# An attention-and-MLP kernel on one core: a diagonal's matmuls as a step of their own, one broadcast by a casting transfer, and a reordered opening list

## The chip, the core and the metric

The kernel runs on one core of one Trainium2 chip. The core has engines that each work through an instruction queue of their own, in order, and wait for one another by semaphores: PE (TensorE, matmuls), DVE (VectorE), ACT (ScalarE), POOL (GpSimd) and SP (SyncE, which here only issues transfers). DMA engines move data between memory and the core. The metric is device time in microseconds (us), from the start to the end of one execution; lower is better.

## What is computed

The reference has two parts. The first is a linear attention with a decay `w` for each head and channel and a bonus `u` for the current token, over 4 sequences of 768 tokens, 8 heads of 48 channels:

```python
for t in range(S):
    cur = einsum('bhd,bhe->bhde', u[None] * k[t], v[t])
    y[t] = einsum('bhd,bhde->bhe', r[t], state + cur)
    state = w[None, :, :, None] * state + einsum('bhd,bhe->bhde', k[t], v[t])
```

The second takes y, with the heads side by side, as x of 3072 tokens by 384 columns: `h = x @ w_in` (384 by 2048), `g = maximum(0.01 * h, h)`, `out = g @ w_out` (2048 by 384).

## The kernel before

**Stages.** The tokens are cut into 24 stages of 128 tokens (n = 0 to 23); four consecutive stages are the same chunk of the four sequences. Inside a chunk the recurrence becomes matrix products: scaled copies of r and k are turned (channels onto partitions), a 128 by 128 score matrix is made for each head and masked, and y is the scores times v, plus r times the state carried from the chunk before, plus a diagonal term, in which each token's v is multiplied by the sum of r, k and u over the channels. Two stages make a pair m, whose 256 tokens go through the MLP together. From m = 3 on (stages 6 and later in the MLP, 10 and later in the attention) a loop emits the work; everything before is emitted in the order of a hand-written list, the string ORDER.

**The list.** Each word in ORDER emits one step, with the number of its stage:

- `k`, `r`, `v`: load of one 128 by 384 piece, from fp32 in memory to bf16 on the chip, issued by POOL (line 223); `wi`, `wo`: load of a quarter of w_in or w_out, also by POOL (lines 233 and 237). k0 and r0 alone go by ACT and SP.
- `P`: DVE multiplies r (`q`) or k (`k`) by its decay table into qk (line 353). `T`: PE turns one half of qk with four matmuls (line 407). `t`: the copy of it from PSUM to tp, by ACT (line 421), or by DVE where `@` stands behind (line 419). `X8T` to `X11T`: for these stages a DMA transpose issued by SP takes the place of T and t (line 358).
- `A`: the scores, 8 matmuls into two PSUM banks (line 432). `M`: the mask, by DVE, one bank at a time (line 441; line 445 from stage 8 on).
- `X` with a number alone: DVE's product of the two halves of tp (line 368); `D`: its sums over channels, four small matmuls (line 460), into spare columns of the PSUM bank that y will use; `Q`: for stages 0 to 7 DVE multiplies v by these sums into vs (line 375). From stage 8 on `q` is DVE's three operations on r, k and the table u_tab (lines 382, 384, 386), and `Q` is two multiplications of the identity by POOL (line 393), which put the sums on the diagonal of the score tile before the mask is applied.
- `Y`: the sum of y in PSUM (line 566); for stages 0 to 7 it begins with three matmuls of vs with the identity (line 559). `y`: ACT's copy of it to xT (line 580).
- `K`: k times v (line 473); `S`: DVE's new state from it (lines 531, 534, 536).
- `G n.g` and `g`: a quarter of the first MLP product for one stage, 12 matmuls (line 605), and ACT's leaky ReLU of it (line 615). `J m.j` and `j`: an eighth of it for a pair of stages, 6 matmuls of 256 columns (line 628), and its ReLU (line 638). `H`: the second product for one stage, 16 matmuls of 384 columns (line 652); `h`: ACT's copy (line 664) and the store, issued by SP (line 666).
- `F`: fills, matmuls of ones whose result nobody reads (line 261), as many as the number says.
- The rest makes the tables: `w`, `w8`, `u8`, `u` are small loads by SP; `bc`, `lnw`, `qtab`, `ktab` the decay tables; `id8`, `wu8`, `Cm`, `Wl`, `C`, `W` the columns of w and of w times u; `u16`, `U`, `utab` a cast of the row u by ACT (line 326), a matmul that spreads it over the partitions (line 330), and a copy to u_tab by ACT (line 335).

**What sets the order.** A step's place in ORDER is its place in its engine's queue, and nothing moves it later. The class Sched notes for each step which buffers it reads and writes, and makes it wait for the steps before that wrote or read them. PSUM has eight banks; a step that needs one takes the one that has been free longest, so it also waits for the copy that freed it. There are no priorities: a step that waits holds everything behind it on its engine. The loads that are needed first in the loop, those of stages 12 and 13, stand at the end of the list; the loop's own loads are held back to a step of the MLP, those of the list are not.

After the list PE's first step is J3.0, the first eighth of the MLP for stages 6 and 7.

Of the kernel before, what the change touches and what calls it, by code (L numbers as in the profile page):

```python
# [17 lines left out]
HD = H * D  # L18
# [109 lines left out]
def bass_rwkv5_eagle__then__act_leaky_relu_kernel(  # L128
# [13 lines left out]
    def SB(name, shape, dt=BF16):  # L142
        return ctx.enter_context(nc.sbuf_tensor(name, shape, dt))
# [180 lines left out]

    def u_cast():
        add("act", lambda: A.activation(u_row16[:, :], u_row[:, :], AF.Copy), R=["u_row"], W=["u_row16"])

    def u_spread():
        ps_u, key = u_bank["u"] = take()
        add("pe", lambda: PE.matmul(ps_u[:, 0:HD], ones[0:1, 0:128], u_row16[:, :], start=True, stop=True),  # L330
            R=["ones", "u_row16"], W=[key])

    def u_table():
        ps_u, key = u_bank["u"]
        add("act", lambda: A.activation(u_tab[:, :], ps_u[:, 0:HD], AF.Copy), R=[key], W=["u_tab"])
        give(key)

    u_bank, c_bank = {}, {}
    at_bank, kv_bank, y_bank = {}, {}, {}
# [199 lines left out]
    def y_mm(n, ps_y, key):  # L539
        it, ia, iv, is_ = n % NTP, n % NAT, n % NVS, n % NT  # L540

# [13 lines left out]
        def emit():  # L555
            whole = n < DIAG
            if whole:
                for s in range(NSL):
                    PE.matmul(ps_y[:, 128 * s:128 * s + 128], vs[iv][:, 128 * s:128 * s + 128], ident[:, :],  # L559
                              start=s == 0, stop=False)  # L560
            columns = [sum((strip(s, q) for s in range(NSL)), []) for q in range(4)]
            for step in range(max(len(x) for x in columns)):
                for q in range(4):
                    if step < len(columns[q]):
                        s, a, m = columns[q][step]
                        last = PE.matmul(ps_y[32 * q:32 * q + 32, 128 * s:128 * s + 128], a, m,  # L566
                                         start=not whole and step == 0, stop=step == len(columns[q]) - 1)
# [90 lines left out]
    def g2_out(n, c0=0, c1=HD):  # L658
# [135 lines left out]
```

## Time and profile before

| | us |
|---|---|
| runs (3): median, lowest, highest | 171.94, 170.69, 172.17 |
| span of the profiled execution, first to last instruction | 168.6 |
| PE busy in it | 163.7 |
| DVE busy | 106.9 |
| POOL busy | 103.6 |
| ACT busy | 90.8 |
| PE's first matmul of J3.0, that is, the end of the list | 53.36 |

The span is the profiled execution's own time as the profile shows it; the page gives no device time beside it. The median of the runs is 3.3 us longer than the span; what lies around the first and the last instruction is not in the trace. Times in the trace are counted from the first instruction. A matmul's row is longer than its share of PE, because matmuls overlap: the distance from one group's start to the next is what a group costs. Durations in the chain of waits are such distances already.

### The profile page before, as it was taken

The page shows a single profiled execution, that of the slowest core. Times are in us where ns is not written, and L with a number is a line of the kernel's source. Part 1 is how long each engine was busy: PE and PEld are TensorE (multiplying, and loading weights), DVE is VectorE, ACT ScalarE, POOL GpSimd, SP SyncE. Part 2 cuts the span into 40 slices and gives each one's busy share as a digit, 9 for nine tenths or more (in the row PEclk, how much of TensorE's full clock was granted, in tenths as well). Part 3 has the DMA queues.
Part 4 walks back from the last instruction along what each step waited for, and adds up shares of the span by engine and source line. Part 5 has one row for each costly group of instructions (what it writes and reads, how often), then busy time and mean ns, then how long its engine had stood idle before and what let it go on. Part 6 is the DMA issues. An engine that isn't in the chain of part 4 may idle for free.

```text
span 168.6 us, 5011 instructions
## 1 busy us (share of the span) xinstructions
PE 163.7 (97%) x2170; PEld 126.1 (75%) x2170; DVE 106.9 (63%) x217; ACT 90.8 (54%) x167; POOL 103.6 (61%) x117
## 2 busy tenths in 40 slices
PE   6899999999999999999999999999999999999994
PEld 4787898988667867867867867768768668668663
DVE  6599799874583999869959959969876050000000
ACT  3837866886123933933834735735637538449221
POOL 7999999990249998994993993993708100000000
PEclk9999999999999999999999999999999999999999
DMA  6999999999999959999599399299241011011012
GB/s 99 142 151 165 170 167 173 182 184 148 130 167 187 163 75 144 155 118 173 71 140 167 64 141 177 71 132 193 59 121 47 0 51 47 0 51 47 29 68 95
DMA packets 99148, 19.67 MB, mean 117 GB/s; under 512 B 92339, under 2 KB 99126, under 8 KB 99126
## 3 DMA queue, kind: packets, MB, share of 16 engines
q0 software_dynamic: 76512, 10.03, 92.1%
q1 hardware_dynamic: 21574, 9.12, 23.2%
q8 instruction: 17, 0.28, 0.7%
q10 hardware_dynamic: 1040, 0.20, 0.6%
q14 instruction: 5, 0.04, 0.1%
HBM read 20.45 MB, written 4.72 MB: 149 GB/s over the span
## 4 chain that ended last, share of the span: by engine, by line
PE 89%; POOL 5%; DMA 4%; issue 0%; ACT 0%; POOLq 0%
PE ps L652 37%; PE ps L628 31%; PE ps L605 6%; PE ps L566 6%; DMA w_in_sb<-in_moe_w_in_dram 4%; PE ps L432 4%; PE ps L473 2%; POOL k_sb L223 2%; POOL r_sb L223 2%; PE ps L407 1%; POOL v_sb L223 1%; PE ps L559 1%; PE ps L261 0%; POOL w_in_sb L233 0%; PE ps L460 0%
## 5 line engine op out<-in xcount | busy, mean ns | idle before, releaser
L652 PE MATMUL ps<-w_out_sb,gT 128*128 128x384 bf16 (+2 forms) x400 | 65.7, 320 | 0.0
L628 PE MATMUL ps<-xT,w_in_sb 128*128 128x256 bf16 x480 | 54.7, 273 | 0.0
L652 PEld LDWEIGHTS ps<-w_out_sb,gT 128*128 128x128 bf16 x400 | 37.9, 98 | 22.0
L393 POOL TENSOR_TENSOR at<-ident,s_tok 128x512 bf16<-128x512 bf16 x32 | 35.0, 1121 | 26.9 <-DVE s_tok L386 26.9
L628 PEld LDWEIGHTS ps<-xT,w_in_sb 128*128 128x128 bf16 x480 | 46.6, 98 | 6.4 <-ACT xT L580 0.2
L638 ACT ACTIVATE gT<-ps 128x512 bf16<-128x512 f32 x80 | 47.8, 597 | 6.4 <-PE ps L628 1.6
L664 ACT ACTIVATE out_sb<-ps 128x384 f32<-128x384 f32 (+2 forms) x25 | 11.9, 478 | 52.9 <-PE ps L652 52.9
L445 DVE CAST_PREDICATED at<-mask,ps 128x512 bf16<-128x512 uint16 x32 | 19.8, 684 | 18.0 <-PE ps L432 18.0
L223 POOL DMA_DIRECT2D v_sb<-in_v_dram x24 | 22.9, 955 | 0.0
L223 POOL DMA_DIRECT2D k_sb<-in_k_dram x23 | 21.5, 965 | 0.4 <-issue 0.4
L223 POOL DMA_DIRECT2D r_sb<-in_r_dram x23 | 21.2, 930 | 0.0
L353 DVE TENSOR_TENSOR qk<-r_sb,qtab 128x384 bf16<-128x384 bf16 x23 | 14.2, 617 | 3.8 <-DMA r_sb<-in_r_dram 3.8
L353 DVE TENSOR_TENSOR qk<-k_sb,ktab 128x384 bf16<-128x384 bf16 x23 | 13.0, 570 | 1.3 <-DMA k_sb<-in_k_dram 1.3
L580 ACT ACTIVATE xT<-ps 128x384 bf16<-128x384 f32 x24 | 11.0, 491 | 4.8 <-PE ps L566 4.8
L605 PE MATMUL ps<-xT,w_in_sb 128*128 128x128 bf16 x192 | 12.5, 219 | 0.4 <-DMA w_in_sb<-in_moe_w_in_dram 0.4
L615 ACT ACTIVATE gT<-ps 128x512 bf16<-128x512 f32 x16 | 9.6, 597 | 5.3 <-PE ps L605 4.9
L605 PEld LDWEIGHTS ps<-xT,w_in_sb 128*128 128x128 bf16 x192 | 11.0, 98 | 0.8 <-DMA w_in_sb<-in_moe_w_in_dram 0.5
L384 DVE TENSOR_TENSOR rku<-r_sb,ku 128x384 bf16<-128x384 bf16 x16 | 10.8, 675 | 0.6
L566 PE MATMUL ps<-at,v_sb 128*32 128x128 bf16 x384 | 10.8, 220 | 0.0
L534 DVE TENSOR_TENSOR sum_t<-ps,st 128x384 bf16<-128x384 f32 x16 | 8.8, 551 | 2.7 <-PE ps L473 2.7
L441 DVE TENSOR_TENSOR at<-ps,mask 128x512 bf16<-128x512 f32 x16 | 10.3, 681 | 0.3 <-PE ps L432 0.3
L261 PE MATMUL ps<-ones 128*128 128x128 bf16 x69 | 8.5, 257 | 1.3 <-DVE ones L251 1.3
(60 smaller groups left out, 135.1 us busy)
## 6 DMA issues: line engine op xcount, KB each, us to landing
out_dram<-out_sb SPq DMA_DIRECT2D x23, 192.0 KB, 3.6
v_sb<-in_v_dram POOLq DMA_DIRECT2D x24, 96.0 KB, 6.3
k_sb<-in_k_dram POOLq DMA_DIRECT2D x23, 96.0 KB, 6.1
r_sb<-in_r_dram POOLq DMA_DIRECT2D x23, 96.0 KB, 5.9
w_in_sb<-in_moe_w_in_dram POOLq DMA_DIRECT2D x4, 384.0 KB, 6.8
w_out_sb<-in_moe_w_out_dram POOLq DMA_DIRECT2D x4, 384.0 KB, 9.3
tp<-qk SPq DMA_TRANSPOSE x16, 2.8
k_f<-in_k_dram ACTq DMA_DIRECT2D x1, 192.0 KB, 2.7
```

The lines of the kernel that those rows point to most:

```text
L223: add("pool", lambda: G.dma_start(dst, src), R=pace, W=[(which, n)], dma=f"{which}{n}")
L353: add("dve", lambda: V.tensor_tensor(qk[iq][:, H * half:H * half + H, 0:D], hd(src), hd(tab[:, :]), ALU.mult), R=[(name, n), "qk"[half] + ...
L384: add("dve", lambda: V.tensor_tensor(rku[i2][:, :], r_of(n), ku[i2][:, :], ALU.mult), R=[("r", n), ("ku", i2)], W=[("rku", i2)])
L393: add("pool", lambda hh=hh, s_of=s_of: G.tensor_tensor(at[ia][:, hh, :, :], ident[:, :].unsqueeze(1).to_broadcast([128, NP, 128]), s_of.un ...
L445: add("dve", lambda: V.copy_predicated(at[n % NAT][:, hh, :, :], mask[:, :].bitcast(mybir.dt.uint16).unsqueeze(1).to_broadcast([128, NP, 1 ...
L566: last = PE.matmul(ps_y[32 * q:32 * q + 32, 128 * s:128 * s + 128], a, m, start=not whole and step == 0, stop=step == len(columns[q]) - 1)
L580: add("act", lambda: A.activation(xT[m % NX][:, :, 128 * half:128 * half + 128], ps_y[:, 0:HD].rearrange("p (s t) -> p s t", t=128), AF.Copy),
L605: last = PE.matmul(ps_g[:, 128 * f:128 * f + 128], w_in_sb[:, s, 128 * fb:128 * fb + 128], xT[ix][:, s, t], start=s == 0, stop=s == NSL - 1)
L628: last = PE.matmul(ps_g[:, 256 * f:256 * f + 256], w_in_sb[:, s, 128 * fb:128 * fb + 128], xT[ix][:, s, :], start=s == 0, stop=s == NSL - 1)
L638: add("act", lambda: A.activation(gT[ig][:, 2 * j:2 * j + 2, :].rearrange("p f t -> p (f t)"), ps_g[:, :], AF.Prelu, alpha=0.01), R=[key], ...
L652: last = PE.matmul(ps_o[:, 0:c1 - c0], gT[ig][:, s, 128 * half:128 * half + 128], w_out_sb[:, s, c0:c1], start=s == 0, stop=s == NFB - 1)
L664: add("act", lambda: A.activation(out_sb[io][:, c0:c1], ps_o[:, 0:c1 - c0], AF.Copy), R=[key], W=held)
```

## The change

Three things change, all of them ahead of the loop.

The three matmuls of vs with the identity leave the step `Y` and become a step `Z`, which can be placed by itself; it waits for vs and the identity, and `Y` for the rest. The row u is no longer loaded by SP, cast by ACT, spread by PE and copied by ACT; POOL issues one transfer that reads the row 128 times and casts it on the way, straight into u_tab. And the list has another order, in which `Z` is new, `u16`, `U` and `utab` are gone, and the fills are 58 in place of 69. The other steps are the same ones.

```diff
 ORDER = """
-w k0 r0 w8 u8 u wlz tcol k1 ones table one exps qk0 r1 v0z r5 F12 bc wi2 lnw id qtab wu8 v0 id8 u16 F13 Cm P0q ktab U
-k3 P1q T0q Wl P0k utab T1q r3 P1k t0q T0k C P5q W T1k t1q@ k4 T5q t0k t1k@ tri t5q F2 A0 X0 v1 X1 F2 A1 M0a F3 D0 wi1
-M0b F5 D1 F1 K0 k5 P3k P3q F11 T3k Q0 r4 F3 T3q P4k t3k F3 Y0 M1b v3 t3q T4k M1a y0 F2 K1 A3 r2 t4k Q1 F1 G0.2 M3a wi3
-F1 Y1 S1 g0.2 G0.1 M3b v5 y1 X3 F2 G1.2 r7 P5k g0.1 S0 T5k g1.2 D3 P4q k6 G1.1 Q3 t5k T4q r6 g1.1 K3 P2q Y3 S3 t4q T2q
-k2 X5 y3 F2 A5 X4 F1 A4 t2q M5a G3.2 v4 M4b F1 G3.3 wi0 g3.2 M4a D4 D5 G0.3 g3.3 k7 M5b G1.3 P7q g0.3 v7 Q5 K5 P6k G3.1
-g1.3 S5 wo2 T6k g3.1 Y5 P6q v2 P2k t6k T6q Q4 y5 r10 F2 K4 T2k t6q@ T7q t2k Y4 v6 t7q@ A6 y4 S4 F1 A2 wo3 G1.0 M6a r11
-F1 J2.7 P7k g1.0 M6b wo0 J2.0 j2.7 M2b J2.6 v8 j2.0 X2 M2a J2.2 j2.6 wo1 K7 J2.1 j2.2 v9 S7 K2 J2.4 j2.1 S2 r9 G0.0
-P10q j2.4 r8 K6 J2.3 g0.0 S6 v11 D2 G3.0 j2.3 X6 Q2 k8 T7k g3.0 D6 J2.5 Q6 t7k k11 Y2 P11q j2.5 X7 A7 k9 y2 Y6 M7a k10
-D7 M7b y6 G2.1 Q7 v10 G2.0 g2.1 G2.3 g2.0 G2.2 g2.3 H1 g2.2 P9q P8q H2 h1 P8k q8 X8T K8 H0 h2 P9k Q8 S8 X9T P10k P11k
-K9 X10T H3 h0 q9 X11T S9 Q9 Y7 h3 A9 y7 A8 M8a M9a M9b M8b k12 r12 v12 k13 r13 v13
+tcol exps ones F1 wlz F12 one k1 r1 F2 k0 table v0z w bc id qk0 lnw r0 ktab w8 F13 r2 id8 u8 wu8 v0 Cm k2 qtab F3 P0k Wl P1k T1k W C P1q T1q T0k P0q
+T0q t0q v1 t1k@ F1 F11 t1q@ tri P2q A1 X1 P2k T2k wi0 D1 F3 M1a t0k A0 T2q F5 X0 D0 Q1 M1b M0b t2q Z1 Y1 Q0 t2k y1 M0a K1 k5 r5 A2 G1.0 k4 Z0 P5k g1.0
+M2b K0 r4 Y0 y0 T5k v2 P5q wi3 F3 X2 M2a T5q t5k v5 wi1 t5q v4 k3 r3 G0.0 D2 F2 P4k P4q T4k K2 g0.0 t4k T4q t4q Q2 v3 F2 S1 X5 Z2 Y2 A5 y2 S0 A4 wi2
+M4a D5 G2.0 M5b G0.3 g2.0 Q5 G1.3 g0.3 X4 G2.3 M4b g2.3 S2 M5a D4 Z5 k7 G2.1 r7 G1.1 K5 G0.1 Q4 Z4 S5 g1.3 P3q Y5 Y4 g1.1 P3k g0.1 T3q y5 K4 y4 T3k K3
+J2.7 r6 k6 J2.2 t3q S3 S4 t3k wo0 A3 M3b J2.0 j2.7 X3 wo2 G2.2 u wo3 wo1 r8 k8 P7q M3a g2.1 J2.3 j2.0 P7k P6q k9 T7q r11 g2.2 r10 j2.2 r9 G0.2 J2.5
+T6q g0.2 P6k v6 v7 T6k j2.5 D3 T7k J2.6 t7k G1.2 t7q@ k11 Q3 t6k t6q@ Z3 Y3 g1.2 A6 y3 X7 A7 J2.1 v9 j2.6 k10 M6b M6a G3.3 G3.0 P8q G3.1 J2.4 P8k j2.3
+v11 g3.3 G3.2 q8 g3.0 M7b g3.1 q9 X6 M7a H0 v10 P10q P9k g3.2 H3 P11q h3 P9q H2 D6 K7 h0 X9T v8 h2 P10k Q9 D7 X8T P11k Q6 K9 Q8 j2.4 H1 Z6 j2.1 S9 K6
+Q7 Z7 S7 h1 Y6 y6 S6 X10T X11T r12 Y7 A9 M9b y7 k13 A8 v13 K8 M8b v12 M8a r13 M9a S8 k12
 """
...
-    u_row = SB("u_row", [1, HD], FP32)
-    u_row16 = SB("u_row16", [1, HD])
...
-    def row(h):
-        return dram(h, 0, [[HD, 1], [1, HD]])
+    def rows(h):
+        return dram(h, 0, [[0, 128], [1, HD]])
...
+    def load_u():
+        add("pool", lambda: G.dma_start(u_tab[:, :], rows(u)), W=["u_tab"], dma="u")
...
     def y_mm(n, ps_y, key):
...
-            if whole:
-                for s in range(NSL):
-                    PE.matmul(ps_y[:, 128 * s:128 * s + 128], vs[iv][:, 128 * s:128 * s + 128], ident[:, :],
-                              start=s == 0, stop=False)
...
-        reads = [("v", n), "v0", ("at", ia, 0), ("at", ia, 1), "ident", ("tp", it, 0)]
-        if n < DIAG:
-            reads.append(("vs", iv))
+        reads = [("v", n), "v0", ("at", ia, 0), ("at", ia, 1), ("tp", it, 0)]
...
+    def y_diagonal(n):
+        ps_y, key = y_bank[n]
+
+        def emit():
+            for s in range(NSL):
+                last = PE.matmul(ps_y[:, 128 * s:128 * s + 128], vs[n % NVS][:, 128 * s:128 * s + 128], ident[:, :],
+                                 start=s == 0, stop=False)
+            return last
+
+        add("pe", emit, R=[("vs", n % NVS), "ident"], W=[key])
```

More of the change, by code (lines that the diff above doesn't have):

```diff
@@ L323, in wu_product @@
             R=["w_head", "u_head"], W=["wu_head"])
[L325 to L338, printed above, removed]
+    def load_u():
+        add("pool", lambda: G.dma_start(u_tab[:, :], rows(u)), W=["u_tab"], dma="u")
+    c_bank = {}
     at_bank, kv_bank, y_bank = {}, {}, {}
@@ L539, in y_mm @@
     def y_mm(n, ps_y, key):
-        it, ia, iv, is_ = n % NTP, n % NAT, n % NVS, n % NT
+        it, ia, is_ = n % NTP, n % NAT, n % NT
         def strip(s, q):
@@ L675, in bass_rwkv5_eagle__then__act_leaky_relu_kernel @@
         "u8": lambda: add("sp", lambda: SP.dma_start(u_head[:, :], by_head(u)), W=["u_head"], dma="u8"),
-        "u": lambda: add("sp", lambda: SP.dma_start(u_row[:, :], row(u)), W=["u_row"], dma="u"),
+        "u": load_u,
         "one": lambda: add("dve", lambda: V.memset(one_row[:, :], 1.0), W=["one_row"]),
@@ L681, in bass_rwkv5_eagle__then__act_leaky_relu_kernel @@
         "Cm": columns_mm, "Wl": log_columns, "C": decay_columns, "W": decay_table,
-        "u16": u_cast, "U": u_spread, "utab": u_table,
     }
@@ L689, in bass_rwkv5_eagle__then__act_leaky_relu_kernel @@
         "Q": lambda n, x: scaled_v(n) if n < DIAG else diag_tile(n), "q": lambda n, x: row_sums(n),
-        "Y": lambda n, x: y_sum(n), "y": lambda n, x: y_out(n), "K": lambda n, x: kv_mm(n), "S": lambda n, x: state(n),
+        "Z": lambda n, x: y_diagonal(n), "Y": lambda n, x: y_sum(n), "y": lambda n, x: y_out(n), "K": lambda n, x: kv_mm(n), "S": lambda n, x: state(n),
         "G": lambda n, x: g1(n, int(x[1:])), "g": lambda n, x: g1_out(n, int(x[1:])),
```

## The prediction

> **What bounds the kernel now.** I read the page first, then busy time by stretch, then the chain of waits. The page gives the span and the chain that ended last:
>
> ```profile
> span 168.6 us, 5011 instructions
> PE 89%; POOL 5%; DMA 4%; issue 0%; ACT 0%; POOLq 0%
> ```
>
> Busy time by stretch (length, then busy us and count for each engine), from the end of the list to the end of the last J:
>
> ```profile
> 53.36:155.87 102.51, 102.51 (x1290) 77.90 (x1291) 67.30 (x118) 57.25 (x103) 60.84 (x63) 1.00 0.98 101
> ```
>
> After the list PE is busy for all of 102.51 us: there is no slack in which a late start could be won back, so what the list gains or loses goes into the end one for one. Next PE's own rows inside the list (start, length, engine, line, names):
>
> ```profile
> 6.61 0.49 PE L330 MATMUL ps<-u_row,ones 1*128 1x384 bf16 x1
> 7.03 2.31 PE L407 MATMUL ps<-ident,qk 128*128 128x128 bf16 x20
> ...
> 11.59 0.78 PE L261 MATMUL ps<-ones 128*128 128x128 bf16 x11
> 12.20 0.39 PE L407 MATMUL ps<-ident,qk 128*128 128x128 bf16 x4
> ...
> 14.59 0.83 PE L605 MATMUL ps<-xT,w_in_sb 128*128 128x128 bf16 x12
> ...
> 16.34 0.84 PE L605 MATMUL ps<-xT,w_in_sb 128*128 128x128 bf16 x12 [0.35 <-DMA w_in_sb<-in_moe_w_in_dram]
> ```
>
> The reader is to see that PE is nearly full from about 7 us on, and that its one marked wait after the first G is 0.35 us for a piece of w_in. A fill costs (12.20 - 11.59) / 11 = 0.055 us, the spread of u 7.03 - 6.61 = 0.42.
>
> **The change part by part: PE's work.** Prices of PE's steps, from the chain of waits (start, length, line):
>
> ```profile
> 22.01 0.67 PE ps L605 x12
> 22.68 0.18 PE ps L460 x8
> ...
> 24.22 0.17 PE ps L473 x4
> ...
> 25.06 0.22 PE ps L407 x4
> ```
>
> ```profile
> 36.17 0.68 PE ps L628 x6
> ...
> 37.02 0.34 PE ps L566 x16
> 37.36 0.33 PE ps L432 x8
> 37.69 0.27 PE ps L559 x3
> 37.96 0.51 PE ps L566 x28
> ```
>
> ```profile
> 46.72 2.60 PE ps L652 x16
> ```
>
> So G 0.67, D 0.09, K 0.17, T 0.22, J 0.68, Y 0.34 (0.51 with a carried state), A 0.33, Z 0.27, H 2.60.
>
> The change takes off 11 fills (0.6), U (0.42) and, since no piece of w_in is now late (below), the 0.35: 1.4 us. Splitting Z from Y removes no matmul. ACT loses two short copies, hidden then as now.
>
> Where the new list puts PE: its first G is G1.0. In the old list the first G began at 14.59 with 58 fills ahead of it, U, two T and one K that now come later: 14.59 - 7 x 0.055 - 0.42 - 2 x 0.22 - 0.17 = 13.2, if DVE keeps up. It does not quite. A2 takes the bank that M0b frees, and between P2k and A2 DVE has P2k, M1a, X0, Q1, M1b and M0b. k2 is now the fifth transfer of POOL, issued at about 5.4, and a load near the start takes 4.3, so P2k starts at about 9.7:
>
> ```profile
> k_sb<-in_k_dram POOLq DMA_DIRECT2D x1, 96.0 KB, 4.3
> ```
>
> ```profile
> 10.31 1.28 DVE L441 TENSOR_TENSOR at<-ps,mask 128x512 bf16<-128x512 f32 x2
> ```
>
> With 0.6 for a mask and some 0.35 for each of the others, plus a wait of about 0.4 for A1, M0b ends near 13.2, A2 at 13.6, and G1.0 starts at 13.75 (bounds: 13.2, and 14.6 if one of these loads is one place later). From G1.0 to the end of the list PE has 16 G, 8 J, 4 H, 10 T, 9 K, 7 A, 6 D, 7 Z, 3 short and 4 long Y and 7 fills: 10.72 + 5.44 + 10.40 + 2.20 + 1.53 + 2.31 + 0.54 + 1.89 + 3.06 + 0.39 = 38.5. So without new waits the list ends at **52.2**, 1.2 ahead of 53.36.
>
> **The loads.** POOL's queue: the last listed loads, the two-instruction Q steps, then the loads of stages 12 and 13; later the loop's.
>
> ```profile
> 33.39 3.70 POOL L223 DMA_DIRECT2D k_sb<-in_k_dram  x4
> 36.85 1.12 POOL L223 DMA_DIRECT2D v_sb<-in_v_dram  x1
> ...
> 49.57 2.16 POOL L393 TENSOR_TENSOR at<-ident,s_tok 128x512 bf16<-128x512 bf16 x2 [2.11 <-DVE s_tok L386]
> 51.68 0.94 POOL L223 DMA_DIRECT2D k_sb<-in_k_dram  x1
> ...
> 71.99 0.94 POOL L223 DMA_DIRECT2D k_sb<-in_k_dram  x1
> ```
>
> Time to landing of the load at 33.39, and of the last one at 36.85:
>
> ```profile
> k_sb<-in_k_dram POOLq DMA_DIRECT2D x1, 96.0 KB, 10.2
> ```
>
> ```profile
> v_sb<-in_v_dram POOLq DMA_DIRECT2D x1, 96.0 KB, 9.5
> ```
>
> They land at 43.6 and 46.35, with four loads from one to the other: 0.68 each, while POOL issues faster. So the transfers stand in a line, and a place in the line is a time. The new list has the same pieces and u. No row shows u's transfer; it writes as many bytes as a k load, so at most 0.7, at least nothing; I take 0.7, and the last load lands at 47.05. From there backwards: wo1, with 14 loads behind it, at 37.5 (H0 wants it at 38.7, the least cover of all: 1.2); v7 at 43.0 (K7 wants it at 46.5); r9, with 8 behind it, at 41.6. The pieces of w_in come 1 to 4 us before their G. u has 5 us to spare before q8. Stage 3 late and stage 2 early cost nothing on PE by this count.
>
> But r9 sets something else. Q9 and Q8 now stand next to each other in POOL's queue, ahead of r12, and wait for DVE's q9:
>
> ```profile
> 43.93 0.35 DVE L382 TENSOR_TENSOR ku<-k_sb,u_tab 128x384 bf16<-128x384 bf16 x1
> 44.31 0.36 DVE L384 TENSOR_TENSOR rku<-r_sb,ku 128x384 bf16<-128x384 bf16 x1
> 44.70 0.55 DVE L386 TENSOR_REDUCE s_tok<-rku 128x8 f32<-128x384 bf16 x1
> ```
>
> After r9 there is 0.94 to go (44.31 to 45.25): 42.55. Two Q at 51.68 - 49.57 = 2.1 each: POOL issues r12 at **46.8**, where the old list, whose q9 came late, issued its first such load at 51.68. Six loads follow, until about 52.
>
> **The transposes.** SP's queue of the old list, and two of the loop's transposes:
>
> ```profile
> 44.92 2.71 SPq L358 DMA_TRANSPOSE tp<-qk  x1
> 47.68 0.58 SPq L666 DMA_DIRECT2D out_dram<-out_sb  x1
> 48.31 2.66 SPq L358 DMA_TRANSPOSE tp<-qk  x2
> ...
> 71.17 2.62 SPq L358 DMA_TRANSPOSE tp<-qk  x2
> ```
>
> Time to landing: of the first at 48.31, when no load was under way; of the one at 44.92, over the tail of the loads; and of the second of the pair at 71.17, which was issued 0.6 after the load at 71.99:
>
> ```profile
> tp<-qk SPq DMA_TRANSPOSE x1, 2.7
> ```
>
> ```profile
> tp<-qk SPq DMA_TRANSPOSE x1, 4.5
> ```
>
> ```profile
> tp<-qk SPq DMA_TRANSPOSE x1, 5.8
> ```
>
> A transpose that meets loads takes 5.8 in place of 2.7. In the new list SP has h3, h0, X9T, h2, X8T, in this order, and A8 is PE's last step but one. Counting back from 52.2: K8, A8, A9, Y7, Y6, Z7, K6, Z6, H1, K9, D7, K7 and D6 are 5.7, so H2 ends at 46.5, H3 at 43.9, and A8 is due at **51.7**. A copy waits 0.2 for the matmuls' end and takes 0.49:
>
> ```profile
> 46.59 0.49 ACT L664 ACTIVATE out_sb<-ps 128x384 f32<-128x384 f32 x1 [2.11 <-PE ps L652]
> ```
>
> h3 and h0 are copied by 45.1, stored by SP by 45.7, and X9T is issued then. Its nearest row is that at 44.92, also issued over the tail of the loads: 2.7 of SP's time, until 48.4 (the other rows say 1.3: 47.0). Then h2's store, 0.6, and X8T at 49.05 (47.85). Both are after r12's 46.8, so it meets the loads: landing at 54.85 (53.65). A8 starts at 54.9 in place of 51.7, K8 and J3.0 stand behind it on PE, and the list ends at 55.4: 2.0 later than 53.36 (with the short issue 54.2: 0.85 later; with the long issue and 4.5 to land, 0.75). I take the long issue, whose row is the nearer one. X9T lands by 51.5 even at 5.8, just when A9 is due; X10T and X11T have until 60.
>
> [...]
>
> **The rivals.** *The transpose is in time* (faster): r12 is issued after X8T, or X8T loses only a share of the engines. This decides at 51.7: X8T has to land by then, from 49.05 in 2.7 and from 47.85 in 3.9. Then the list ends at 52.2 and the gain of 1.2 stays: 170.7. For it: no row shows a transpose issued more than 0.6 after a row of loads began. Against it: 5.8 in the loop, and 2 us between r12 and X8T. *PE's clock rises later*: the 20 matmuls at 7.03 stand 2.1 / 20 = 0.107 apart, the fills at 11.59 0.055. If the new head, with its waits for DVE, holds the slow pace up to about 16, the 1.1 us of steps from G1.0 to there doubles: 1.1 on top of the 2.0, 175.0. For it: fewer fills between the same waits. [...] *A load is late*: wo1 has 1.2 of cover; past it H0 and all behind it wait, and X8T with them.
>
> **How the numbers follow.** The sum is made in the profiled execution, span 168.6; the median of the runs, 171.94, lies 3.3 above it, and I leave that alone: 171.94 + 2.0 = 173.9, put at 174.0. Late transpose 0.62, its own range 172.7 to 174.7, six tenths of it above 173.7; in time 0.18, around 170.7, a third of it below 170.2; clock as well 0.10; anything else 0.10, evenly spread. One per cent, 1.7 us, is about what a measurement of this kernel can tell from no change: slower by more 0.37 + 0.10 + 0.03 = 0.50, faster by more 0.06 + 0.03 = 0.09, within 0.41. The range 170.7 to 175.2 leaves out half of the case in time and half of the clock's.
>
> **What would show it.** PE idle before A8 (line 432) for 2 to 3 us, ended by the transpose; POOL's first load after two Q at about 46.8; X8T issued at 48 to 49 with over 5 to land; G1.0 at about 13.75; no wait of G for w_in. I am wrong if A8 starts at about 51.7, or if PE stands still for long before H0.

## The result, and the profile after

The changed kernel takes 177.99 us (median of four runs, 177.53 to 178.40) against 171.94: a ratio of 1.037, interval 1.032 to 1.042, or 6.05 us more. The forecast was 174.0 with a range up to 175.2: the sign was right, the size a third of what came. Some of the later runs, four of the kernel before and one of another kernel, lay over 1.5 per cent above the fastest run of their kernel, and the medians, ranges and ratios below leave them out.

The profiled execution of the changed kernel took 178.07 us, 1.8 more than its span. By the same 1.8 the profiled execution of before, span 168.6, belongs to a run of about 170.4, near the fastest of its runs and not near their median. So the spans differ by 7.7, the medians by 6.05, and the 1.6 between is where the two profiled executions lie among their runs.

The page of the changed kernel: span, clock row, chain and transposes.

```profile
span 176.3 us, 4989 instructions
...
PEclk9999999999997599999999999999999999999999
...
PE 91%; DMA 5%; DVE 1%; issue 1%; ACT 1%; POOL 0%; SPq 0%; POOLq 0%; DVEq 0%
...
tp<-qk SPq DMA_TRANSPOSE x16, 5.5
```

Two things are new: a slice and a half in which TensorE's clock was half granted, and transposes that take 5.5 in the median (2.8 in before). Next PE's rows in the list (start, length in us, line, names, and in brackets the idle time before and what ended it):

```profile
13.92 0.83 PE L596 MATMUL ps<-xT,w_in_sb 128*128 128x128 bf16 x12
...
38.86 7.96 PE L643 MATMUL ps<-w_out_sb,gT 128*128 128x384 bf16 x48
...
50.95 0.34 PE L562 MATMUL ps<-ident,vs 128*128 128x128 bf16 x3 [0.65 <-DVE vs L361]
...
54.00 0.40 PE L418 MATMUL ps<-tp 48*128 48x128 bf16 x8 [1.81 <-DMA tp<-qk]
59.00 0.61 PE L418 MATMUL ps<-tp 48*128 48x128 bf16 x8 [4.60 <-DMA tp<-qk]
...
59.85 3.42 PE L619 MATMUL ps<-xT,w_in_sb 128*128 128x256 bf16 x19
```

G1.0 starts at 13.92 and H0 at 38.86, as the count had them. Then A9 (at 54.00) waits 1.81 for X9T, A8 (at 59.00) 4.60 for X8T, and J3.0 starts at 59.85 where before it started at 53.36. The chain of waits, in order of time, says what A8 hung on:

```profile
50.00 0.50 ACT out_sb L655
...
50.63 8.23 DMA tp<-qk
...
59.00 0.61 PE ps L418 x8
```

ACT copies the end of H2 at 50.00, SP stores it, SP issues X8T at 50.63, and X8T takes 8.23. Busy time by stretch has the clock (start and end, length, busy us and count of PE, PEld, DVE, ACT and POOL, granted clock, DMA share, GB/s):

```profile
55.43:62.25 6.82, 3.25 (x24) 2.35 (x25) 2.50 (x5) 0.60 (x1) 0.00 (x0) 0.50 1.70 143
```

For 6.82 us the clock stood at 0.50; 3.25 of them PE worked. The wait for X8T thus cost a second time, in the matmuls behind it.

The time of a kernel can be split by two numbers: the start of J3.0, which is the end of the list, and the rest of the span.

| kernel | J3.0 starts | span | rest |
|---|---|---|---|
| before | 53.36 | 168.6 | 115.2 |
| changed | 59.85 | 176.3 | 116.5 |
| loads behind X8T (first experiment) | 55.71 | 172.7 | 117.0 |
| changed, fills in the waits | 60.65 | 175.9 | 115.3 |
| loads behind X8T, 40 fills | 54.58 | 169.9 | 115.3 |
| Q9 late | 52.58 and 51.95 | 167.9 and 167.2 | 115.3 |

Where the clock did not fall, the rest is 115.2 to 115.3, with one exception (116.2, in the experiment with the old u below, where the last store made the difference). So of the 7.7 the rest holds 1.2, and the list 6.5. These 6.5 are 1.81 + 4.60 of waits and 0.5 for A8 and K8, most of it the half clock, less 0.4 by which the list was shorter: A9 could have begun at 54.00 - 1.81 = 52.2, and with 0.74 for A9, A8 and K8, as in the Q9 experiment below, J3.0 would have come at 52.9.

Why X8T was issued so late and landed so late stands in the queues. POOL, DVE and SP of the changed kernel:

```profile
43.92 4.43 POOL L379 TENSOR_TENSOR at<-ident,s_tok 128x512 bf16<-128x512 bf16 x4 [5.50 <-DVE s_tok L372]
48.30 0.94 POOL L219 DMA_DIRECT2D r_sb<-in_r_dram  x1
```

```profile
45.14 1.20 DVE L339 TENSOR_TENSOR qk<-k_sb,ktab 128x384 bf16<-128x384 bf16 x1
46.26 2.31 DVE L339 TENSOR_TENSOR qk<-r_sb,qtab 128x384 bf16<-128x384 bf16 x2
```

```profile
44.78 0.85 SPq L657 DMA_DIRECT2D out_dram<-out_sb  x2
48.60 1.36 SPq L344 DMA_TRANSPOSE tp<-qk  x1
50.01 0.58 SPq L657 DMA_DIRECT2D out_dram<-out_sb  x1
50.63 1.29 SPq L344 DMA_TRANSPOSE tp<-qk  x1
```

SP stored h3 and h0 by 45.6, as forecast. But X9T also needs the products P9k and P9q (line 339), and DVE ended the last of them at 48.57: beside POOL's Q9 and Q8 (43.92 to 48.35) such a product takes 1.2 us (0.35 in the experiment with Q9 late below). X9T follows at 48.60, h2's store and X8T behind it. Meanwhile POOL issues r12 at 48.30, so that X9T too meets the loads; time to landing of X9T:

```profile
tp<-qk SPq DMA_TRANSPOSE x1, 5.3
```

### The profile page after: what moved, and what is told of

It reads as the page before. It is cut to its first block, busy times and chain, and to the rows that moved or that the text cites. A ratio compares the mean times of both kernels' runs of the same rounds, so it can differ in the third digit from the quotient of the medians.

```text
span 176.3 us, 4989 instructions
## 1 busy us (share of the span) xinstructions
PE 164.9 (94%) x2158; PEld 126.8 (72%) x2158; DVE 110.3 (63%) x217; ACT 89.2 (51%) x165; POOL 104.2 (59%) x118
## 4 chain that ended last, share of the span: by engine, by line
PE 91%; DMA 5%; DVE 1%; issue 1%; ACT 1%; POOL 0%; SPq 0%; POOLq 0%; DVEq 0%
PE ps L643 36%; PE ps L619 30%; PE ps L596 6%; PE ps L548 5%; DMA tp<-qk 5%; PE ps L418 4%; PE ps L257 3%; PE ps L459 2%; PE ps L393 2%; PE ps L562 1%; PE ps L297 1%; DVE at L427 0%; ACT out_sb L655 0%; PE ps L446 0%; DVE prod L354 0%
## 5 line engine op out<-in xcount | busy, mean ns | idle before, releaser
L619 PE MATMUL ps<-xT,w_in_sb 128*128 128x256 bf16 x480 | 56.2, 276 | 0.0
L619 PEld LDWEIGHTS ps<-xT,w_in_sb 128*128 128x128 bf16 x480 | 47.1, 99 | 6.9
L219 POOL DMA_DIRECT2D v_sb<-in_v_dram x24 | 22.4, 963 | 0.0
L339 DVE TENSOR_TENSOR qk<-r_sb,qtab 128x384 bf16<-128x384 bf16 x23 | 16.6, 724 | 3.3 <-DMA r_sb<-in_r_dram 3.3
L418 PE MATMUL ps<-tp 48*128 48x128 bf16 x192 | 8.4, 224 | 6.4 <-DMA tp<-qk 6.4
L339 DVE TENSOR_TENSOR qk<-k_sb,ktab 128x384 bf16<-128x384 bf16 x23 | 13.9, 606 | 0.4 <-DMA k_sb<-in_k_dram 0.3
L418 PEld LDWEIGHTS ps<-tp 48*128 48x128 bf16 x192 | 5.7, 97 | 9.7 <-issue 9.1
L596 PEld LDWEIGHTS ps<-xT,w_in_sb 128*128 128x128 bf16 x192 | 11.2, 98 | 0.3 <-DMA w_in_sb<-in_moe_w_in_dram 0.2
```

The lines of the kernel that those rows point to most:

```text
L219: add("pool", lambda: G.dma_start(dst, src), R=pace, W=[(which, n)], dma=f"{which}{n}")
L339: add("dve", lambda: V.tensor_tensor(qk[iq][:, H * half:H * half + H, 0:D], hd(src), hd(tab[:, :]), ALU.mult), R=[(name, n), "qk"[half] + ...
L418: last = PE.matmul(at_bank[n][hh][0][:, 128 * p:128 * p + 128], tp[it][rows, NP + p, :], tp[it][rows, p, :], start=True, stop=True)
L596: last = PE.matmul(ps_g[:, 128 * f:128 * f + 128], w_in_sb[:, s, 128 * fb:128 * fb + 128], xT[ix][:, s, t], start=s == 0, stop=s == NSL - 1)
L619: last = PE.matmul(ps_g[:, 256 * f:256 * f + 256], w_in_sb[:, s, 128 * fb:128 * fb + 128], xT[ix][:, s, :], start=s == 0, stop=s == NSL - 1)
```

## The experiments

The theory: X8T is slow because the loads of stages 12 and 13 are under way beside it; it is late because Q9 stands beside the products; the wait costs once more through the clock. Rivals: X8T is slow for its own sake in this place; it is SP's place in the queue that counts; Z or u's transfer costs. Each kernel was run in several rounds against the kernel before; the ratios below are to that kernel in the same session. Its medians were 171.42 (loads behind X8T, Q9 late, fills in the waits, loads early), 171.29 (the 40 fills, Z, u, old u) and 171.06 (X8T early, without Z, Q9 late again), against 171.94 beside the changed kernel; so differences between two sessions, and to the 177.99, hold to about 1 us.

**The loads wait for X8T.** Loads of stages 12 and 13 get X8T as a further input:

```diff
+    def held(n):
+        return [("tp", 8 % NTP, 0)] if n >= 12 else ()
...
-        "r": lambda n, x: load_first(n, "r") if n < EXACT else load_one(n, "r"),
+        "r": lambda n, x: load_first(n, "r") if n < EXACT else load_one(n, "r", held(n)),
...
```

> The kernel after, with the six loads of stages 12 and 13 held until the transpose X8T has landed; nothing else moved. Theory (the transposes are late because these loads are under way beside them): X9T, issued at 48.6, lands in about 2.8 us in place of 5.3, X8T, issued at 50.6, in about 2.8 in place of 8.2, that is at 53.4; A8 starts at 53.5 in place of 59.0, PE's clock stays at full rate, J3.0 starts near 54.0 (after: 59.85; before: 53.36), time near 172.5. Rival (the transposes are late by themselves: issued late, behind the stores of h0 and h2): they still take over 5 us, A8 starts after 57, time 176 or more.

174.35 us (173.99 to 174.78), ratio 1.014 (1.007 to 1.021): 3.6 less than the changed kernel, but not the whole way. PE's rows, the clock, and the queues of the DMA engines from X8T's issue until it landed (packets, MB, share of the engines):

```profile
55.19 0.40 PE L418 MATMUL ps<-tp 48*128 48x128 bf16 x8 [3.00 <-DMA tp<-qk]
```

```profile
56.23:59.64 3.41, 3.41 (x18) 2.43 (x17) 3.31 (x9) 1.55 (x3) 3.41 (x5) 0.50 1.59 135
```

```profile
q1 hardware_dynamic: 1800, 0.76, 118.2%
q8 instruction: 1, 0.02, 2.1%
```

```profile
tp<-qk SPq DMA_TRANSPOSE x1, 4.8
```

With no packet of a load beside it X8T took 4.8 in place of 8.2, so the loads are worth 3.4. X9T, issued at 48.27, landed in 2.9, like the 2.7 of a transpose alone in before. What else held X8T? The only other queue at work is the one named instruction: one packet of 16 KB, begun at 52.03, 1.6 us long (2.1% of 16 engines for 4.8 us). Such a packet is called an instruction fetch here; that it brings PE's instructions is the author's reading, from the count of the packets (in the last section) and the next experiment. And A8's wait of 3.00 again took the clock: 3.41 us at 0.50, all of them work, 1.7 lost.

**The same with 40 fills ahead of J2.7.** The 40 matmuls are meant to shift the moment of this fetch; they cost 40 x 0.055 = 2.2 by the price of a fill, and PE, which is full, has nothing to hide them under. The loads wait as in the first experiment.

```diff
-M4a D5 G2.0 M5b G0.3 g2.0 Q5 G1.3 g0.3 X4 G2.3 M4b g2.3 S2 M5a D4 Z5 k7 G2.1 r7 G1.1 K5 G0.1 Q4 Z4 S5 g1.3 P3q Y5 Y4 g1.1 P3k g0.1 T3q y5 K4 y4 T3k K3
+M4a D5 G2.0 M5b G0.3 g2.0 Q5 G1.3 g0.3 X4 G2.3 M4b g2.3 S2 M5a D4 Z5 k7 G2.1 r7 G1.1 K5 G0.1 Q4 Z4 S5 g1.3 P3q Y5 Y4 g1.1 P3k g0.1 T3q y5 K4 y4 T3k K3 F40
```

> The kernel of the first experiment (loads of stages 12 and 13 held until X8T has landed), with 40 fills more on PE ahead of J2.7. Theory (in that experiment X8T took 4.8 us with no load under way because a 16 KB instruction fetch of 1.6 us fell on it at 52.0): the fills move this fetch ahead by 80 PE instructions, to about 46 us, clear of X8T; X8T is issued some 2.2 us later, near 52.5, and lands in 2.7 to 3.0; PE waits for it under 1.2 us, so the clock stays at full rate; J3.0 starts at 55.5 to 56.0 as there, and the time is 172.2 to 173.2 in spite of 2.2 us more of work. Rival (X8T takes 4.8 for another reason, such as the stores beside it): A8 starts near 57.3, time 176 to 177.

171.74 us (171.36 to 172.34), ratio 1.001 (0.997 to 1.006): 2.6 faster than without the fills, although PE has 2.2 more to do, and half a microsecond below what was expected. From X9T's issue to X8T's, and then from X8T's issue until it landed:

```profile
q8 instruction: 1, 0.02, 2.8%
...
tp<-qk SPq DMA_TRANSPOSE x1, 4.2
```

```profile
q1 hardware_dynamic: 1736, 0.59, 83.9%
...
tp<-qk SPq DMA_TRANSPOSE x2, 2.7
```

```profile
53.85 0.62 PE L418 MATMUL ps<-tp 48*128 48x128 bf16 x16
```

The fetch was expected near 46, ahead of both. It fell on X9T, which took 4.2 in place of 2.9, and X8T without it took 2.7 in place of 4.8. A9 and A8 ran together without a wait and the clock stayed up (rest of the span 115.3 in place of 117.0). So an instruction fetch in the middle of a transpose that has no loads beside it cost 1.3 and 2.1 here.

The same can be seen in two traces that were there before. The first is the kernel before: the transpose at 44.92, whose 4.5 the prediction read as the price of the loads' tail. From its issue until it landed the loads moved 0.02 MB, and one fetch stood beside it:

```profile
q0 software_dynamic: 211, 0.02, 8.3%
...
q8 instruction: 1, 0.02, 2.3%
```

The second is X8T in the changed kernel, from 50.7 to 58.9. The loads moved 0.37 MB in this time (0.25 MB beside the transpose of the loop that took 5.8), and after its fetch all queues together nearly stood still for about 1 us (each number is GB/s over a slice of 0.205 us; slices 25 to 30, from 55.6 to 56.9):

```profile
GB/s 135 134 144 154 154 154 157 164 215 188 176 162 207 197 192 258 253 137 145 154 157 274 212 128 31 2 7 10 9 37 232 217 155 146 206 205 208 257 248 161
...
q0 software_dynamic: 3946, 0.37, 92.1%
...
q8 instruction: 1, 0.02, 0.7%
```

By this reading about 1 of the 8.2 is the fetch's. No run took the fetch away and left the loads in place, so this share is argued, not shown.

**Q9 behind P11k.** One move in the changed list, of q9 and Q9, neither the loads nor SP's queue touched:

```diff
-v11 g3.3 G3.2 q8 g3.0 M7b g3.1 q9 X6 M7a H0 v10 P10q P9k g3.2 H3 P11q h3 P9q H2 D6 K7 h0 X9T v8 h2 P10k Q9 D7 X8T P11k Q6 K9 Q8 j2.4 H1 Z6 j2.1 S9 K6
+v11 g3.3 G3.2 q8 g3.0 M7b g3.1 X6 M7a H0 v10 P10q P9k g3.2 H3 P11q h3 P9q H2 D6 K7 h0 X9T v8 h2 P10k D7 X8T P11k q9 Q9 Q6 K9 Q8 j2.4 H1 Z6 j2.1 S9 K6
```

> The kernel after with one step moved: DVE's q9 (and with it Q9, whose place in POOL's queue stays the same) from ahead of X6 to behind P11k. Theory: q9 ends near 48, POOL's Q9 and Q8 run from 48 to 52.2, so the loads of stages 12 and 13 begin at about 52 in place of 48.3, as in the kernel before (51.7). The transposes X9T and X8T are then issued ahead of them, at about 46 and 48 to 49, and land by 50 and 52; A8 waits less than 0.5 us, J3.0 starts at 52.5 to 53.0, time 171.0 to 171.6. Rival (lateness of the transposes by themselves): X9T is issued some 2.5 us earlier, X8T with it, but still takes over 5: A8 near 56, time near 174.5.

169.30 us (168.98 to 169.63), ratio 0.984 (0.977 to 0.991): 8.7 below the changed kernel, below what was expected, and faster than before by 1.6 per cent. DVE, POOL, SP and PE:

```profile
42.94 0.35 DVE L339 TENSOR_TENSOR qk<-k_sb,ktab 128x384 bf16<-128x384 bf16 x1
43.20 0.62 DVE L339 TENSOR_TENSOR qk<-r_sb,qtab 128x384 bf16<-128x384 bf16 x2
```

```profile
47.82 4.28 POOL L379 TENSOR_TENSOR at<-ident,s_tok 128x512 bf16<-128x512 bf16 x4 [9.39 <-PE ps L446]
52.05 0.94 POOL L219 DMA_DIRECT2D r_sb<-in_r_dram  x1
```

```profile
46.21 1.33 SPq L344 DMA_TRANSPOSE tp<-qk  x1
...
48.31 1.32 SPq L344 DMA_TRANSPOSE tp<-qk  x1
```

```profile
51.84 0.62 PE L418 MATMUL ps<-tp 48*128 48x128 bf16 x16
...
52.58 5.40 PE L619 MATMUL ps<-xT,w_in_sb 128*128 128x256 bf16 x48
```

Both ends of the squeeze are gone: the products take 0.35 with POOL idle beside them, X9T and X8T are issued 2.4 and 2.3 earlier, and r12 3.75 later, at 52.05, when X8T (landed in 3.0, at 51.3) is through. PE waits for neither. The same kernel was run once more in the last session:

> The kernel of the second experiment once more, beside the one without Z on the same chip: 169.0 to 169.8, faster than the kernel before by 1 to 2 per cent.

169.15 us (168.97 to 169.28), ratio 0.987 (0.981 to 0.993), with J3.0 at 51.95. It beats the changed kernel by far, and the one before by 1.3 per cent, in an interval that leaves out no difference.

**X8T early in SP's queue.** Only X8T is moved, ahead of H3's store; Q9 and the loads stay as in the changed kernel.

```diff
-v11 g3.3 G3.2 q8 g3.0 M7b g3.1 q9 X6 M7a H0 v10 P10q P9k g3.2 H3 P11q h3 P9q H2 D6 K7 h0 X9T v8 h2 P10k Q9 D7 X8T P11k Q6 K9 Q8 j2.4 H1 Z6 j2.1 S9 K6
+v11 g3.3 G3.2 X8T q8 g3.0 M7b g3.1 q9 X6 M7a H0 v10 P10q P9k g3.2 H3 P11q h3 P9q H2 D6 K7 h0 X9T v8 h2 P10k Q9 D7 P11k Q6 K9 Q8 j2.4 H1 Z6 j2.1 S9 K6
```

> The kernel after, with one step moved: X8T in SP's queue from behind h2's store to ahead of h3's, so that it is issued near 40.5, over the listed loads and 8 us ahead of r12 (48.3). Theory (A8 waits for nothing but X8T, and X8T for the loads of stages 12 and 13): X8T is slow, 7 to 9 us beside the listed loads, but lands by 49.5, A8 starts right behind A9; A9 still waits for X9T (issued 48.6, landing near 53.9); J3.0 at 54.7 to 55.0 in place of 59.85, PE's wait is under 2 us and its clock stays at full rate; time 172.3 to 173.3. Rival (PE's late start has another cause besides, behind X8T): time 175 or more.

171.13 us (170.69 to 171.61), ratio 1.001 (0.998 to 1.004): 6.9 below the changed kernel, more than expected. X8T took 6.7 in the line of the listed loads, but had from 39.6 on to do it. What is left is X9T's wait:

```profile
52.94 0.62 PE L418 MATMUL ps<-tp 48*128 48x128 bf16 x16 [1.55 <-DMA tp<-qk]
```

J3.0 followed at 53.67. The 1.55 did not take the clock (span 169.0, rest 115.3). So it is X8T alone that makes A8 late; what a transpose costs depends on when its result is due, not only on how long it takes.

**Fills in the two waits.** PE is kept busy with 30 fills ahead of A9 and 80 ahead of A8; the transposes stay as they are.

```diff
-Q7 Z7 S7 h1 Y6 y6 S6 X10T X11T r12 Y7 A9 M9b y7 k13 A8 v13 K8 M8b v12 M8a r13 M9a S8 k12
+Q7 Z7 S7 h1 Y6 y6 S6 X10T X11T r12 Y7 F30 A9 M9b y7 k13 F80 A8 v13 K8 M8b v12 M8a r13 M9a S8 k12
```

> The kernel after, with 30 fills put on PE ahead of A9 and 80 ahead of A8, which run while PE would wait for the transposes. Theory (the fall of PE's clock to half from 55.4 to 62.3 us is a cost of its own, 1.2 to 1.6 us, on top of the wait): PE's granted clock stays at full rate, A8 still starts near 59.0, span 174.7 to 175.1, time 176.4 to 176.8. Rival (the clock costs nothing, all of it is the wait): time 178.0.

176.73 us (175.76 to 177.66), ratio 1.027 (1.019 to 1.035): 1.26 less than the changed kernel with 110 matmuls more.

```profile
52.16 1.85 PE L257 MATMUL ps<-ones 128*128 128x128 bf16 x30
54.00 0.40 PE L418 MATMUL ps<-tp 48*128 48x128 bf16 x8
54.33 2.74 PE L257 MATMUL ps<-ones 128*128 128x128 bf16 x46
58.15 2.06 PE L257 MATMUL ps<-ones 128*128 128x128 bf16 x34 [1.08 <-issue]
60.15 0.40 PE L418 MATMUL ps<-tp 48*128 48x128 bf16 x8
```

The clock stayed at 1.00 and the rest of the span was 115.3 in place of 116.5, although J3.0 came 0.8 later: the fills lasted until 60.2, with 1.08 of idle time in them that the row puts down to issue, while X8T landed at 59.0. The clock's share is thus 1.2 in the rest, and some 0.35 in A8 and K8 (0.85 from A8's start to J3.0's in the changed kernel, 0.50 here).

**The loads early in the old list.** The kernel before, with the loads of stages 12 and 13 moved to behind v10, so that its transposes meet them:

```diff
-D7 M7b y6 G2.1 Q7 v10 G2.0 g2.1 G2.3 g2.0 G2.2 g2.3 H1 g2.2 P9q P8q H2 h1 P8k q8 X8T K8 H0 h2 P9k Q8 S8 X9T P10k P11k
-K9 X10T H3 h0 q9 X11T S9 Q9 Y7 h3 A9 y7 A8 M8a M9a M9b M8b k12 r12 v12 k13 r13 v13
+D7 M7b y6 G2.1 Q7 v10 k12 r12 v12 k13 r13 v13 G2.0 g2.1 G2.3 g2.0 G2.2 g2.3 H1 g2.2 P9q P8q H2 h1 P8k q8 X8T K8 H0 h2 P9k Q8 S8 X9T P10k P11k
+K9 X10T H3 h0 q9 X11T S9 Q9 Y7 h3 A9 y7 A8 M8a M9a M9b M8b
```

> The kernel before, with the loads of stages 12 and 13 moved in POOL's queue from behind Q9 to directly behind the load v10; nothing else moved. Theory: the line of loads then runs until about 50.5 in place of 46.4, over the issue of X8T (44.9) and X9T (48.3); both take over 5 us to land in place of 4.5 and 2.7, A9 and A8 (due at 52.7 and 53.0) wait 0.5 to 3 us, time 172.5 to 175. Rival (loads beside transposes cost nothing here; something else in the new list makes them late): time as before, 171.9.

172.98 us (171.85 to 174.22), ratio 1.006 (1.001 to 1.012). The trace has four transposes issued at 47.51, 50.20, 52.14 and 54.60, which land in 6.2, 5.0, 3.9 and 2.8; the last load lands at 53.2. The times fall as the loads run out, but this proves less than it seems. Beside the first the loads moved 0.21 MB, and an instruction fetch fell on it too; from the issue of the second until it landed they moved 0.01 MB, so the second and third were held by something other than the loads' bytes, perhaps by the first, which landed at 53.7. The price in time is small, and it can't be read from the end of the list: J3.0 came at 55.95 without a marked wait. The list itself was late from its head on, as its eleven fills show:

```profile
12.91 1.37 PE L261 MATMUL ps<-ones 128*128 128x128 bf16 x11
```

In the profiled execution of before these eleven took 0.78. So this experiment agrees with the theory, does not prove it, and leaves open how much of the 0.6% is the transposes'.

**Z alone, and u's transfer alone, in the old list.** In the first, each Y of stages 0 to 7 gets its Z directly ahead of it; in the second u comes by POOL ahead of wo3, and the two casts and the spread go:

```diff
-M0b F5 D1 F1 K0 k5 P3k P3q F11 T3k Q0 r4 F3 T3q P4k t3k F3 Y0 M1b v3 t3q T4k M1a y0 F2 K1 A3 r2 t4k Q1 F1 G0.2 M3a wi3
...
+M0b F5 D1 F1 K0 k5 P3k P3q F11 T3k Q0 r4 F3 T3q P4k t3k F3 Z0 Y0 M1b v3 t3q T4k M1a y0 F2 K1 A3 r2 t4k Q1 F1 G0.2 M3a wi3
...
```

> The kernel before, with the three matmuls of vs as a step Z directly ahead of each Y, and nothing else. Theory: nothing is gained or lost by the step itself, time within 0.5 us of the kernel before. Rival (the split costs: another semaphore wait at each of eight places on PE): 0.1 to 0.2 us each, 1 to 1.5 us slower.

```diff
-w k0 r0 w8 u8 u wlz tcol k1 ones table one exps qk0 r1 v0z r5 F12 bc wi2 lnw id qtab wu8 v0 id8 u16 F13 Cm P0q ktab U
...
+w k0 r0 w8 u8 wlz tcol k1 ones table one exps qk0 r1 v0z r5 F12 bc wi2 lnw id qtab wu8 v0 id8 F13 Cm P0q ktab
...
-g1.3 S5 wo2 T6k g3.1 Y5 P6q v2 P2k t6k T6q Q4 y5 r10 F2 K4 T2k t6q@ T7q t2k Y4 v6 t7q@ A6 y4 S4 F1 A2 wo3 G1.0 M6a r11
+g1.3 S5 wo2 T6k g3.1 Y5 P6q v2 P2k t6k T6q Q4 y5 r10 F2 K4 T2k t6q@ T7q t2k Y4 v6 t7q@ A6 y4 S4 F1 A2 u wo3 G1.0 M6a r11
...
```

> The kernel before, with u brought by POOL's casting transfer (in its queue ahead of wo3) in place of the row load, the cast, the spread on PE and the copy; nothing else. In the kernel after this transfer held the line of loads for 1.6 us (wo2 landed at 33.3, u at 34.9), where I had put 0.7. Theory: all loads behind it land 1.6 later, so the transposes come later by as much; PE saves 0.4; the sum is -0.4 to +0.8, time 171.5 to 172.8. Rival (the transfer is free, PE's saving stays): 171.5 or less, with the last listed load landing at 46.4 as before.

Z: 170.78 us, ratio 1.000 (0.995 to 1.004). u: 171.62 us, ratio 1.002 (0.997 to 1.007). Neither part moves the time by itself. In the line of loads u takes 1.5 (landings at 32.58 and 34.05), twice the 0.7 of a k load, and in the changed kernel 1.6 (33.30 and 34.89).

**Q9 late with the old u, and Q9 late without Z.** Both start from the kernel with Q9 behind P11k; the first has u as before (SP's row, ACT's casts, PE's spread), the second Z merged into Y again.

```diff
-tcol exps ones F1 wlz F12 one k1 r1 F2 k0 table v0z w bc id qk0 lnw r0 ktab w8 F13 r2 id8 u8 wu8 v0 Cm k2 qtab F3 P0k Wl P1k T1k W C P1q T1q T0k P0q
-T0q t0q v1 t1k@ F1 F11 t1q@ tri P2q A1 X1 P2k T2k wi0 D1 F3 M1a t0k A0 T2q F5 X0 D0 Q1 M1b M0b t2q Z1 Y1 Q0 t2k y1 M0a K1 k5 r5 A2 G1.0 k4 Z0 P5k g1.0
+tcol exps ones F1 wlz F12 one k1 r1 F2 k0 table v0z w bc id qk0 lnw r0 ktab w8 F13 r2 id8 u8 u wu8 v0 Cm k2 qtab u16 F3 P0k Wl P1k T1k W C P1q T1q T0k P0q
+T0q t0q v1 t1k@ F1 F11 t1q@ tri P2q A1 X1 P2k T2k wi0 D1 F3 M1a t0k A0 T2q F5 X0 D0 Q1 M1b M0b t2q U Z1 Y1 Q0 t2k utab y1 M0a K1 k5 r5 A2 G1.0 k4 Z0 P5k g1.0
...
```

> The kernel of the second experiment (q9 and Q9 behind P11k), with u brought as in the kernel before: row load by SP, cast and copy by ACT, spread by one matmul on PE. Theory: PE pays 0.1 to 0.4 for the spread, and the line of loads is 1.6 us shorter, which here nothing waits for: time 169.3 to 169.9. Rival (the 1.6 us in the line of loads are worth something even here): 168.5 to 169.0.

```diff
-T0q t0q v1 t1k@ F1 F11 t1q@ tri P2q A1 X1 P2k T2k wi0 D1 F3 M1a t0k A0 T2q F5 X0 D0 Q1 M1b M0b t2q Z1 Y1 Q0 t2k y1 M0a K1 k5 r5 A2 G1.0 k4 Z0 P5k g1.0
...
+T0q t0q v1 t1k@ F1 F11 t1q@ tri P2q A1 X1 P2k T2k wi0 D1 F3 M1a t0k A0 T2q F5 X0 D0 Q1 M1b M0b t2q Y1 Q0 t2k y1 M0a K1 k5 r5 A2 G1.0 k4 P5k g1.0
...
```

> The kernel of the second experiment (q9 and Q9 behind P11k), with the three matmuls of vs back in Y. Theory: the separate step is worth little in this list too, within 0.5 us of that kernel. Rival (Z is what lets this list run without waits, PE using the time in which the mask is made): 1 us or more slower than it.

Old u: 170.04 us (169.56 to 171.41), ratio 0.995 (0.991 to 0.998). Without Z: 169.90 us (169.12 to 170.41), ratio 0.991 (0.987 to 0.995). Both stand some 0.75 above the two results of the kernel they start from, 169.30 and 169.15, and both lie outside what was expected: the old u just above its range, the kernel without Z between theory and rival. For Z this compares kernels of one session, and its J3.0 came at 52.89 against 51.95. For u the profiled execution doesn't bear it out: J3.0 stood at 52.14, between 51.95 and 52.58. Its span, 168.3, was 1.1 longer than the shorter of the two; 0.2 of it is the list, and 0.9 lies in the last store, which took 2.4 to land in place of 1.5. So Z is worth some 0.4% here, and u's worth stays open.

## Why the prediction was off

In short: the step that failed is X8T, the largest term of the sum. It was to be issued at 49.05 and to land in 5.8; it was issued at 50.63 and landed in 8.2, 4.0 later in all. Next to it stands a term that the sum put at nothing: the half clock that the wait brings, 1.6. Span against span the forecast was short by 5.7, and these two make up nearly all of it.

The mechanism was the one forecast: A8, last but one on PE, waits for X8T, X8T meets the loads of stages 12 and 13, and those come early because Q9 and Q8 stand together in POOL's queue. Moving Q9 alone takes the loss away, and so do holding the loads (with the fetch moved) and issuing X8T earlier. The signs that were named came too: a wait of PE before A8 ended by the transpose, G1.0 at 13.92 (forecast 13.75), no wait of G for w_in, H0 at 38.86 (38.7). Held against the forecast, point by point:

- **The order by itself, -1.2: right.** With its transposes in time the list gives 169.15 to 169.30, 1.2 below the profiled run of before, the base of the sum, and 1.9 to 2.1 below the medians of before in those sessions. Z cost nothing, as forecast, and u's shorter path on PE was not late for anybody.
- **X8T issued at 49.05: 1.6 too early.** The path to X9T was counted through SP and the stores of h3 and h0 only, and these were done in time. The products P9k and P9q were not counted: the prices of DVE were taken from rows without POOL's arithmetic beside them. 1.20 and 2.31 for three products, beside POOL's four in 4.43, stand against 0.35 and 0.62 where Q9 was moved away. X9T was so issued 2.9 late, at 48.60 in place of 45.7. A second error took back 1.3 of it: the 2.7 of SP's time for X9T, the "long issue", came out at 1.36, the value that the other rows had.
- **r12 at 46.8: 1.5 too early.** The line of loads was 1.1 to 1.3 later than its count (r9 landed at 42.73 against 41.6, the last listed load at 48.30 against 47.05), mostly u's 1.6 where 0.7 was taken "at most". A broadcast load was priced by its bytes, and it took twice that. This error worked the other way, but not enough to help X8T.
- **X8T in 5.8: the failed step, 8.2.** Its row was a poor neighbour: the transpose of the loop had 0.25 MB of loads beside it. In this place 0.37 MB of loads, X9T, h2's store and an instruction fetch stood beside it. The first experiment showed the loads' part, 3.4; it and the one with 40 fills showed what a fetch costs a transpose that has no loads beside it, 1.3 to 2.1. How much of the 8.2 the fetch made with the loads there too (it began at 55.08) was not separated; the trace shows about 1 us in which next to nothing moved. The row of 4.5 at 44.92, the prediction's other neighbour, was misread: what stood beside it was a fetch and hardly any loads.
- **A9 in time at 51.5: no, 1.81 late.** X9T was issued 2.9 later than forecast, and so met r12 and the loads behind it (5.3 to land).
- **The clock: not in the sum.** The rival in which the clock rises later was put at the head of the list, where two matmuls stood 0.107 apart and later 0.055. There the pace doubled on time, at about 11 (10.2 in before). The trace's first record of the granted clock, at 1.00, begins at that moment, and the view by stretch reads 1.00 ahead of it as well (9.1 to 11.0; 7.0 to 9.1 in before), so a lower clock at the head is not shown. What the forecast wait itself does to the clock was not priced at all. The waits for A9 and A8 lowered it for 6.82 us and cost 1.2 in the rest and 0.35 ahead of it, as the fills in the waits show.
- **The base.** The 2.0 were added to the median, although the profiled execution that they were worked out in stood 1.6 below it. This hid part of the error: span against span the forecast was 2.0 and the result 7.7.

In sum, waits of 6.4 where 3.2 were forecast, 1.7 for the half clock and the steps around it where nothing was, and a list shorter by 0.4 and not 1.2 by the end (Z7 waited 0.65 for DVE, whose products were late): 6.4 + 1.7 - 0.4 = 7.7.

## What to carry to other kernels

Price an instruction by a row in which the neighbour that it will have was at work too (DVE's product took 1.2 us beside POOL's and 0.35 without them), and follow every input of a transfer, not only the queue that issues it. When a forecast ends in a wait of TensorE, add what the wait does to the clock behind it (here some 1.6 us behind waits of 1.81 and 4.60; a wait of 1.55 left the clock up). A transfer that the next step waits for should be issued early enough for the time that it takes beside other transfers (X8T 8.2 us beside the loads, 2.7 with neither a load nor a fetch beside it), or what can wait should be moved behind it: here one small move of Q9, an instruction of another engine, was worth 8.7 us.

## What the runs showed of the hardware

- **Two transposes with an instruction fetch beside them were slower.** The queue named instruction moved 17 packets of 16 KB in the changed kernel, one for every 254 matmuls and weight loads (4316 / 17), 0.9 to 1.4 us each (1.6 in the first experiment). Transposes with no loads beside them in whose middle one fell took 4.8 and 4.2 in place of 2.7 and 2.9. Not every fetch does this: one that began 2.6 after the issue of X8T in the first run with Q9 late left it at 3.0, and beside 0.25 MB of loads, in the loop of the changed kernel, the transpose issued at 92.28, with one begun 5.2 after its issue, took 5.8, as did those at 79.95 and 116.95 without one.
- **The clock fell at a wait of 3.00 us and not at one of 1.55.** After 3.00 us without work (first experiment) the clock was at 0.50 for 3.41 us, after 1.81 and 4.60 with eight matmuls between them for 6.82, twice that; after 1.55 it stayed up.
- **The head of the old list has two speeds.** The eleven fills ahead of Q0 took 0.78 in the profiled execution of before, 1.15 in the one with Z alone, 1.37 in those with u's transfer and with the loads early, and J3.0 came at 53.36, 54.12, 55.07 and 55.95. One fill stood 0.055 us from the next in the first of these and 0.106 in the last two. The view by stretch gives a granted clock of 1.00 from 10 to 16 in the first and in the one with the loads early, so it doesn't show the two speeds. Runs of before also lie between 170.3 and 173.0 us, while those of the kernel with Q9 late lie within 0.7. That the moment at which the pace doubles makes this scatter fits the rows, but no experiment tried it.
